# Later places for z transposes, v's split, the routing gate and the first block table in a fused attention, MLP and mixture-of-experts kernel

## The chip, the cores and the metric

One core of a Trainium2 chip. The metric is the device time of one execution in microseconds (us). TensorE (PE) does the matmuls and transposes, with a weight loader of its own (PEld); VectorE (DVE), ScalarE (ACT) and GpSimd (POOL) do the elementwise work; SyncE (SP) issues most DMAs, GpSimd the indirect ones. Every engine runs its own instructions in program order.

## What is computed

Three stages over 8 batches of 3072 rows of 256 columns, all float32:

```
scores = (z @ z.T) / S                     # z: 3072 x 64 in each batch
x      = u * (relu(scores)**2 @ v)         # attention
h      = x @ w_in                          # 256 -> 2048
x      = (h - tanh(h)) @ w_out             # 2048 -> 256
e      = argmax(x @ w_gate)                # 8 experts, one for each row
gate   = softmax(x @ w_gate)[e] * sigmoid((x @ w_output_gate)[e])
out    = gate * (relu(x @ w1[e]) @ w2[e])  # 256 -> 1024 -> 256
```

To keep float32's precision, each operand of most products is split into a high part (rounded to the matmul's type) and a low part (operand minus high part), and three products (high by high, high by low, low by high) are summed.

## The kernel before

**Stages.** The rows go in 48 chunks of 512 (NCH; 6 in a batch, NG). Chunk c has twelve steps p (NJP), each over 256 keys: `s_mm` (scores into PSUM), `s_relu` (relu and square, ScalarE), `s_split` (high part "a" on VectorE, or on ScalarE for p=1 and 7; low part on GpSimd for p=0, 2, 4, 6, 8, 9, 10, else on VectorE) and `av_mm` (times v). Then `x_make` multiplies by the transposed u and splits x. The MLP of chunk c-1 runs between the steps of chunk c: for each of eight blocks f of w_in and w_out, `wi_mm` (h into PSUM), `g_first`, `g_second`, `g_third` (h - tanh h, by ScalarE and VectorE) and `wo_mm`. Chunk c-2 is then routed, also between the steps of chunk c: `x2_split`, `g_mm` (logits), `route1` (argmax, one-hot), `route2` (positions: five small matmuls "prs", a copy "cum", then six VectorE instructions, among them the cast to whole numbers "pi", L577), `route_gate` (two Exps on ScalarE, L538 and L543, and seven small VectorE instructions), `rows_out` (the rows with their gate to DRAM), `ids_out` (four indirect DMAs that put row numbers into a table sorted by expert). When all chunks are routed, blocks of one expert's rows are gathered and multiplied; the first 39 blocks have 512 rows, the rest 256. The table that tells each block its expert and start is made in two halves by `block_table` from single-partition VectorE work: `table_counts`, `table_steps`, `table_expert` (eight times), `table_out`.

**Order.** No planner: every function is entered by `at(t, fn, ...)` with a time written out by hand (in `SCHED` and the loops), all entries are sorted by that time, and the instructions are issued in this order. So a later time moves a function behind others on every engine's queue that it uses, SP's and GpSimd's too. A chunk is 88 of these units long, a step 7.33. `gap(c, k)` is the time 3.4 units into step k of chunk c.

**Around the change.** In the last chunk of each batch (c = 11, 17, ...) the next batch's z and v come in: `z_load`, `z_split` (GpSimd), `z_tr` (four transposes, then a ScalarE copy to t1, L312), `v_load`, `v_split` (high part on ScalarE, L332; low part on GpSimd, L336). PSUM holds one score tile ("sc"), one h tile and the accumulators; the score tile is also used by `z_tr`, by `u_tr` (the transposes of u, after the scores of p=8), by `g_mm` and by `route2`. The order of a mid-batch chunk c around the routing, before the change:

```
s_mm(c,6) s_relu(c,6) route_gate(c-2) rows_out(c-2) wi_mm(c-1,3,0) s_split(c,6) route2(c-2)
wi_mm(c-1,3,1) ids_out(c-2,0) av_mm(c,5) e_load g_first(c-1,3) s_mm(c,7) wo_mm(c-1,2,0)
g_second(c-1,3) s_relu(c,7) wo_mm(c-1,2,1) g_third(c-1,3) s_split(c,7) av_mm(c,6) wi_mm(c-1,4,0)
s_mm(c,8) s_relu(c,8) wi_mm(c-1,4,1) s_split(c,8) g_first(c-1,4) u_tr(c)
```

`g_third(c-1,2)` stands ahead of this, so its four VectorE instructions come before those of route_gate. The functions that the diff touches, with the lines of the profile:

Of the kernel before, what the change touches and what calls it, by code (L numbers as in the profile page):

```python
# [21 lines left out]
LGC = 128  # L22

SCHED = dict(
    TC=88.0, LA=1.8, EX=3.4, UT=8, ZS=12.0, ZL=(1, 2, 7, 9, 11, 13), M0=0.5, HI=2.5, LG=1.45,
    HA=((1, 3, 5, 7, 9, 11), (1, 2, 4, 5, 7, 8, 10, 11), (1, 7)), LP=((), (6, 8, 10), (0, 2, 4, 6, 8, 9, 10)),
    G2=3.0, G3=5.0, GT=180.0, CT=((16.0, 23.0), (36.0, 43.0), (56.0, 63.0), (76.0, 83.0), (98.4, 102.0), (110.5, 120.4), (131.5, 142.4), (153.5, 155.4)),
    CP=(34.5, 54.5, 74.5, 98.3, 109.4, 131.4, 149.0, 164.3),
# [36 lines left out]
def build(tc, u, v, z, w_in, w_out, w_gate, w_ogate, w1, w2, out):  # L65
# [5 lines left out]
    E = w_gate.shape[1]  # L71
    F2 = w1.shape[2]
    NG = S // CH
    NCH = B * NG
    NJP = S // 256
# [17 lines left out]
    def at(t, fn, *a):  # L93
        tasks.append((t, len(tasks), fn, a))
# [59 lines left out]
    with ExitStack() as st:  # L154
# [53 lines left out]
        T1, T4, V, UT, X, X2, AVP, XP, WS = {}, {}, {}, {}, {}, {}, {}, {}, {}  # L208
        RR, AA, HH, GG, ROWS, LG, GT = {}, {}, {}, {}, {}, {}, {}
# [387 lines left out]
        K = SCHED  # L597
        TC = K["TC"]
        DJ, DF = TC / NJP, TC / NFP
        LA = K["LA"] * DJ  # L600
        EX = K["EX"]

        def gap(c, k):

            c, k = c + k // NJP, k % NJP
            return c * TC + k * DJ + EX

        T_ROUTED = {}
        for b in range(B):
            for g in range(NG):  # L610
                if b == 0:
                    tz = -60.0 + g * K["Z0"]
                    tzt, tv = tz + 2, K["VT"][g]
                else:
                    t0 = (b * NG - 1) * TC
                    tzt, tv = gap(b * NG - 1, K["ZL"][g]), t0 + (2 * g - 1) * DJ + LA + 3.0
                    tz = tzt - K["ZS"]
                at(tz - 9 if b else -75.0 + g, z_load, b, g)
                at(tz, z_split, b, g)
                at(tzt, z_tr, b, g)  # L620
                at(tv - (12 if b else 20 if g else 10), v_load, b, g)
                at(tv, v_split, b, g)
# [9 lines left out]
        for n, c in enumerate([c for c in range(3, NCH - 3) if c % NG != NG - 1][: 4 * E]):  # L632
            t = c * TC + K["ES"]
            at(t - 20.0, e_load, n // 4, n // 2 % 2, n % 2)
            at(t, e_split, n // 4, n // 2 % 2, n % 2)
        for c in range(NCH):
            t0 = c * TC
            at(t0 - (14 if c else 45), t4_make, c)
            at(t0 + TC / 4, u_load, c)
            at(gap(c, K["UT"] * NJP // 12), u_tr, c)  # L640
            for p in range(NJP):
                t = t0 + p * DJ
                at(t, s_mm, c, p)
                at(t + 1.0, s_relu, c, p)
                at(t + 3.0, s_split, c, p)
                at(t + LA, av_mm, c, p)
            end = c == NCH - 1
            at(t0 + TC + LA + 3.0 + K["XM"] if end else t0 + (TC - DJ) + LA + 3.0, x_make, c)
            tm0 = t0 + TC + LA + K["M0"]
            for f in range(NFP):  # L650
                t = tm0 + f * DF
                at(t - (22 if c else 10), ws_load, c, f)
                for i in range(2):
                    at(t + i * K["HI"], wi_mm, c, f, i)
                    lag = K["LG"] * DF + i * K["HI"]
                    if c == NCH - 2 and f == NFP - 1:

                        lag = tm0 + TC + K["W7"] + 0.1 * i - t
                    at(t + lag, wo_mm, c, f, i)
                at(t + K["HI"] + 1.5, g_first, c, f)  # L660
                at(t + K["HI"] + K["G2"], g_second, c, f)
                at(t + K["HI"] + K["G3"], g_third, c, f)
            te = tm0 + (NFP - 1 + K["LG"]) * DF + K["HI"] + 1.5
            if c == NCH - 2:
                te = tm0 + TC + K["W7"] + 1.0
            at(te, x2_split, c)

            n = int((te + 4.0 - EX - t0) // DJ) + 1

            tx, tx1, tx2 = (gap(c, n + h) for h in range(3))  # L670
            tx2 += K["RX"] if end else 0.0
            if c == NCH - 2:

                tx, tx1, tx2 = (t0 + 2 * TC + LA + 3.0 + x for x in K["R6"])
            at(tx, g_mm, c, 0)
            at(tx1, g_mm, c, 1)
            tr = tx1 + (K["R1"] if c == NCH - 2 else 1.5)
            at(tr, route1, c)
            tg = tr + (0.01 if c >= NCH - 2 else 4.0)
            at(tg, route_gate, c)  # L680
            at(tg + 0.5, rows_out, c)
            at(tx2 + (0.5 if c >= NCH - 2 else 1.5), route2, c)

            io = K["IO3"] if c == NCH - 3 else K["IO"]
            for t_ in range(4):
                at(tx2 + (1.0 if c >= NCH - 2 else 2.0) + t_ * io, ids_out, c, t_)
            T_ROUTED[c] = tx2 + 1.0 + 3 * io
# [74 lines left out]
                tt(used[:, 0:E], end, sta, op=ALU.subtract)  # L762

        def block_table(t, half, d):

            at(t, table_counts, half)
            at(t + 2.0 * d, table_steps, half)
            for e in range(E):
                at(t + (4.0 + e) * d, table_expert, half, e)
            at(t + 13.0 * d, table_out, half)  # L770
            return t + 13.0 * d
# [187 lines left out]
        at(170.0, more_consts)  # L959
        at(K["GT"], gates)  # L960
        at(200.0, table_consts)
        t_table = T_ROUTED[NCH - 3] if NA else T_ROUTED[NCH - 1] - 13.0

        block_table(t_table + K["TB0"] - 3 * K["IO3"], 0, K["TBD"])
        t_table = block_table(T_ROUTED[NCH - 1] + 0.2, 1, 1.0)
        tC = NCH * TC + LA + 3.0

        def when(n):

            T, d = K["TS"], 22.0 / (NF2 // 2)  # L970
            k = int(n)
            at_ = lambda k: T[k] if k < len(T) else T[-1] + (k - len(T) + 1) * d
            return tC + at_(k) + (n - k) * (at_(k + 1) - at_(k))

        t0 = when(0)
# [3 lines left out]
        for i in range(NA + NHB):  # L979
            TB = 22.0 if i < NA else 11.0  # L980
            if i == NA:
                t0 = max(t0 + 5.5, t_table + 50.0)
# [33 lines left out]
            t0 = step(NG2) if i + 1 < NA or i >= NA else step(0) + TB  # L1016
# [46 lines left out]
```

## Time and profile before

| | |
|---|---|
| median of 3 runs | 5629.36 us (5626.49 to 5629.8) |
| the profiled execution | 5628.64 us |
| its span, first to last instruction | 5626.9 us |
| TensorE busy | 5564.5 us (99%) |
| VectorE, ScalarE, GpSimd busy | 4255.2, 3576.4, 1794.5 us |
| TensorE's granted clock, mean | 0.997 |

The profile is of one execution. Times in the rows are us from the start of the span. A row of the timeline has start, duration, engine, line of the kernel, operation, output<-inputs with their shapes, the number of instructions merged (x1), and in brackets how long the engine had been idle ahead of it and whose end released it. Matmuls are pipelined, so they overlap in the rows: one of 512 columns lasts 0.39 and the next begins about 0.23 after it.

### The profile page before, as it was taken

What the parts mean: (1) busy time and instruction counts of PE and PEld (TensorE: products, weight loads), DVE (VectorE), ACT (ScalarE), POOL (GpSimd) and SP (SyncE); (2) the same over time, 40 slices, a digit from 0 to 9 for tenths busy, and PEclk for the clock granted to TensorE, in tenths of its full rate; (3) what the DMA queues carried; (4) which work ended last, traced back from release to release, by engine and by line L of the source; (5) the groups of instructions that cost most, each with busy time, mean ns of one, the idle gap of its engine ahead of it and who ended that gap; (6) DMA issues with size and microseconds to landing.
All of it is one profiled execution on the core that took longest, in us unless ns stands there. A gap on an engine that the chain in (4) does not pass through costs nothing. (4 is left out here: it accounts for less than half of the span.)

```text
span 5626.9 us, 71022 instructions
## 1 busy us (share of the span) xinstructions
PE 5564.5 (99%) x26788; PEld 4635.4 (82%) x26788; DVE 4255.2 (76%) x5119; ACT 3576.4 (64%) x3990; POOL 1794.5 (32%) x1170
## 2 busy tenths in 40 slices
PE   8899999999999999999999999999999999999999
PEld 7788888888888888888888888888888888888898
DVE  8788888888888888888888888888888733333344
ACT  8677776777777777767777776777766432223344
POOL 1224222432333233222423332333222233333365
PEclk9999999999999999999999999999999999999999
DMA  6334333333433333334334333333333666666688
GB/s 213 108 123 140 127 129 125 138 128 122 134 130 132 123 131 130 130 120 145 127 119 136 136 125 130 121 141 117 106 113 110 218 223 230 231 232 230 229 298 299
DMA packets 192472, 872.06 MB, mean 155 GB/s; under 512 B 37178, under 2 KB 78272, under 8 KB 128640
## 3 DMA queue, kind: packets, MB, share of 16 engines
q1 hardware_dynamic: 154384, 763.19, 39.2%
q0 software_dynamic: 37312, 103.92, 5.4%
q8 instruction: 213, 3.49, 0.3%
q14 instruction: 131, 1.07, 0.1%
q10 hardware_dynamic: 432, 0.39, 0.0%
HBM read 757.16 MB, written 98.96 MB: 152 GB/s over the span
## 5 line engine op out<-in xcount | busy, mean ns | idle before, releaser
L385 POOL TENSOR_TENSOR a<-r,a 128x1024 fp32r<-128x1024 f32 x325 | 783.9, 2412 | 2578.8 <-DVE a L382 1997.7
L371 ACT ACTIVATE r<-sc 128x1024 f32<-128x1024 f32 x576 | 588.1, 1021 | 943.4 <-PE sc L366 941.2
L432 PE MATMUL h<-x,ws 128*128 128x512 f32 x4608 | 1160.4, 392 | 13.0 <-issue 5.7
L468 PE MATMUL x<-g,ws 128*128 128x512 f32 x4608 | 1150.7, 392 | 2.4 <-DVE g L457 1.4
L432 PEld LDWEIGHTS h<-x,ws 128*128 128x128 f32 x4608 | 862.5, 188 | 199.7 <-issue 11.7
L468 PEld LDWEIGHTS x<-g,ws 128*128 128x128 f32 x4608 | 856.8, 188 | 181.9 <-DVE g L458 5.2
L403 PE MATMUL av<-a,v 128*128 128x512 f32 x2304 | 901.3, 391 | 14.5 <-DVE ut L411 9.8
L404 PE MATMUL av<-a,v 128*128 128x512 f32 x2304 | 898.6, 390 | 0.0
L894 DVE SCALAR_TENSOR_TENSOR hh<-h,hh 128x1024 fp32r<-128x1024 f32 (+1 forms) x248 | 254.6, 1027 | 581.4 <-ACT hh L893 564.7
L372 ACT ACTIVATE r<-r 128x1024 f32<-128x1024 f32 x576 | 611.6, 1062 | 18.3
L406 PE MATMUL av<-a,v 128*128 128x512 f32 x2304 | 616.7, 389 | 2.3 <-POOL a L385 2.3
L882 PE MATMUL h<-xt,b 128*128 128x512 f32 (+1 forms) x2976 | 607.8, 353 | 0.1
L439 DVE TENSOR_TENSOR gd<-h,gd 128x1024 f32<-128x1024 f32 x384 | 468.2, 1219 | 168.7 <-ACT gs L438 168.7
L893 ACT ACTIVATE hh<-h 128x1024 fp32r<-128x1024 f32 (+1 forms) x248 | 215.2, 868 | 592.3 <-PE h L882 440.6
L454 DVE SCALAR_TENSOR_TENSOR gq<-gt,gq 128x1024 f32<-128x1024 f32 x384 | 539.4, 1405 | 54.8 <-ACT gt L449 30.0
L382 DVE CAST a<-r 128x1024 fp32r<-128x1024 f32 x470 | 359.3, 764 | 248.1 <-ACT r L372 163.9
L455 DVE COPY_PREDICATED gq<-gm,gd 128x1024 f32<-128x1024 uint16 x384 | 534.6, 1392 | 13.2
L882 PEld LDWEIGHTS h<-xt,b 128*128 128x128 f32 x2976 | 479.0, 189 | 77.4 <-DVE xt L866 0.5
L403 PEld LDWEIGHTS av<-a,v 128*128 128x128 f32 x2304 | 433.4, 188 | 107.1 <-DVE ut L411 10.2
L406 PEld LDWEIGHTS av<-a,v 128*128 128x128 f32 x2304 | 432.7, 188 | 93.2 <-POOL a L385 3.0
L404 PEld LDWEIGHTS av<-a,v 128*128 128x128 f32 x2304 | 433.4, 188 | 88.9
L458 DVE TENSOR_TENSOR g<-gq,g 128x1024 fp32r<-128x1024 f32 x384 | 476.6, 1241 | 13.1
(158 smaller groups left out, 8570.9 us busy)
## 6 DMA issues: line engine op xcount, KB each, us to landing
ws<-wsd SPq DMA_DIRECT2D x384, 1024.0 KB
b<-wsp SPq DMA_DIRECT2D x102, 2048.0 KB
wsp<-el POOLq DMA_DIRECT2D x32, 1024.0 KB
x2d<-rows SPq DMA_DIRECT2D x48, 576.0 KB
wr<-in_moe_w SPq DMA_DIRECT2D x25, 1024.0 KB
vr<-in_v SPq DMA_DIRECT2D x48, 512.0 KB
ur<-in_u SPq DMA_DIRECT2D x48, 512.0 KB
er<-in_moe_w SPq DMA_DIRECT2D x32, 512.0 KB
```

The lines of the kernel that those rows point to most:

```text
L371: nc.scalar.activation(r, RR.pop((c, p)), AF.Relu, scale=1.0 / S)
L372: nc.scalar.activation(r, r, AF.Square)
L385: eng.tensor_tensor(a[:, 1], r, a[:, 0].bitcast(F32), op=ALU.subtract)
L403: nc.tensor.matmul(dst, vh, a[:, 0, k], start=(J == 0), stop=False)
L404: nc.tensor.matmul(dst, vl, a[:, 0, k], start=False, stop=False)
L406: nc.tensor.matmul(dst, vh, a[:, 1, k], start=False, stop=(J == 2 * NJP - 1))
L432: nc.tensor.matmul(ps, w, x[:, l, k], start=(n == 0), stop=(n == 5))
L454: nc.vector.scalar_tensor_tensor(q, s, pk, q, op0=ALU.add, op1=ALU.mult)
L455: nc.vector.copy_predicated(q, m.bitcast(U16), d)
L458: nc.vector.tensor_sub(gg[:, 1], q, gg[:, 0].bitcast(F32))
L468: nc.tensor.matmul(XP[c][d], w, gg[:, l, i], start=first and n in (0, 2), stop=last and n > 3,)
L882: nc.tensor.matmul(ps[:, j], b1[a][:, k, f * P : (f + 1) * P], xt[:, l, k, 0:W], start=(n == 0 and (W == CH or j == 0)), stop=(n == 3 * ND ...
```

## The change

Five edits of the order; no instruction is added or removed:

- the z transposes of g=2 go from 7 to 7.45 steps into the last chunk of a batch, and with them their load and split (all 3.3 units later);
- `v_load` and `v_split` of a batch's first group (g=0) are 4 units later;
- the last `s_split` (c=47, p=11) is 0.1 later, which puts it behind `g_first(46,6)`;
- `route_gate` and `rows_out` of chunks 0 to 45 are 4.2 units later: behind `s_split(c,6)`, `route2` and the first `ids_out`, `rows_out` also behind an `e_load`, and still ahead of `g_first(c-1,3)`;
- the first half of the block table, spread before over 19.5 units, goes in three lots: counts behind `g_first(46,3)`; steps and experts 0 to 3 behind `g_third(46,3)`; experts 4 to 7 and the output behind `g_first(46,4)`, ahead of `g_third(46,4)`.

With the change the order of the same stretch, and in the last chunk of a batch with z_tr, is:

```
s_mm(c,6) s_relu(c,6) wi_mm(c-1,3,0) s_split(c,6) route2(c-2) wi_mm(c-1,3,1) ids_out(c-2,0)
route_gate(c-2) av_mm(c,5) e_load rows_out(c-2) g_first(c-1,3) s_mm(c,7) wo_mm(c-1,2,0)
g_second(c-1,3) s_relu(c,7) [v_split(b,3)] wo_mm(c-1,2,1) g_third(c-1,3) s_split(c,7) av_mm(c,6)
wi_mm(c-1,4,0) [z_tr(b,2)] s_mm(c,8) s_relu(c,8) ...
```

(before, `z_tr(b,2)` stood behind `s_split(c,7)`, ahead of `av_mm(c,6)`).

```diff
@@ -22,7 +22,7 @@
 LGC = 128
 
 SCHED = dict(
-    TC=88.0, LA=1.8, EX=3.4, UT=8, ZS=12.0, ZL=(1, 2, 7, 9, 11, 13), M0=0.5, HI=2.5, LG=1.45,
+    TC=88.0, LA=1.8, EX=3.4, UT=8, ZS=12.0, ZL=(1, 2, 7.45, 9, 11, 13), M0=0.5, HI=2.5, LG=1.45,
     HA=((1, 3, 5, 7, 9, 11), (1, 2, 4, 5, 7, 8, 10, 11), (1, 7)), LP=((), (6, 8, 10), (0, 2, 4, 6, 8, 9, 10)),
     G2=3.0, G3=5.0, GT=180.0, CT=((16.0, 23.0), (36.0, 43.0), (56.0, 63.0), (76.0, 83.0), (98.4, 102.0), (110.5, 120.4), (131.5, 142.4), (153.5, 155.4)),
     CP=(34.5, 54.5, 74.5, 98.3, 109.4, 131.4, 149.0, 164.3),
@@ -613,7 +613,7 @@
                     tzt, tv = tz + 2, K["VT"][g]
                 else:
                     t0 = (b * NG - 1) * TC
-                    tzt, tv = gap(b * NG - 1, K["ZL"][g]), t0 + (2 * g - 1) * DJ + LA + 3.0
+                    tzt, tv = gap(b * NG - 1, K["ZL"][g]), t0 + (2 * g - 1) * DJ + LA + (3.0 if g else 7.0)
                     tz = tzt - K["ZS"]
                 at(tz - 9 if b else -75.0 + g, z_load, b, g)
                 at(tz, z_split, b, g)
@@ -638,13 +638,13 @@
             at(t0 - (14 if c else 45), t4_make, c)
             at(t0 + TC / 4, u_load, c)
             at(gap(c, K["UT"] * NJP // 12), u_tr, c)
+            end = c == NCH - 1
             for p in range(NJP):
                 t = t0 + p * DJ
                 at(t, s_mm, c, p)
                 at(t + 1.0, s_relu, c, p)
-                at(t + 3.0, s_split, c, p)
+                at(t + (3.1 if end and p == NJP - 1 else 3.0), s_split, c, p)
                 at(t + LA, av_mm, c, p)
-            end = c == NCH - 1
             at(t0 + TC + LA + 3.0 + K["XM"] if end else t0 + (TC - DJ) + LA + 3.0, x_make, c)
             tm0 = t0 + TC + LA + K["M0"]
             for f in range(NFP):
@@ -676,7 +676,7 @@
             at(tx1, g_mm, c, 1)
             tr = tx1 + (K["R1"] if c == NCH - 2 else 1.5)
             at(tr, route1, c)
-            tg = tr + (0.01 if c >= NCH - 2 else 4.0)
+            tg = tr + (0.01 if c >= NCH - 2 else 8.2)
             at(tg, route_gate, c)
             at(tg + 0.5, rows_out, c)
             at(tx2 + (0.5 if c >= NCH - 2 else 1.5), route2, c)
@@ -762,7 +762,13 @@
                 tt(used[:, 0:E], end, sta, op=ALU.subtract)
 
         def block_table(t, half, d):
-
+            if not half:
+                at(tC - 53.2, table_counts, half)
+                at(tC - 49.95, table_steps, half)
+                for e in range(E):
+                    at(tC - (49.9 if e < E // 2 else 42.4) + 0.1 * e, table_expert, half, e)
+                at(tC - 41.5, table_out, half)
+                return tC - 41.5
             at(t, table_counts, half)
             at(t + 2.0 * d, table_steps, half)
             for e in range(E):
@@ -959,11 +965,11 @@
         at(170.0, more_consts)
         at(K["GT"], gates)
         at(200.0, table_consts)
+        tC = NCH * TC + LA + 3.0
         t_table = T_ROUTED[NCH - 3] if NA else T_ROUTED[NCH - 1] - 13.0
 
         block_table(t_table + K["TB0"] - 3 * K["IO3"], 0, K["TBD"])
         t_table = block_table(T_ROUTED[NCH - 1] + 0.2, 1, 1.0)
-        tC = NCH * TC + LA + 3.0
 
         def when(n):
 
```

## Rows read from the trace of the kernel before

**Rows 1.** The page, part 1: busy time, share of the span, instructions.

```profile
PE 5564.5 (99%) x26788; PEld 4635.4 (82%) x26788; DVE 4255.2 (76%) x5119; ACT 3576.4 (64%) x3990; POOL 1794.5 (32%) x1170
```

**Rows 2.** The table of waits: engine, line, waited for: us in total, times, longest.

```profile
ACT sm L543 <- DVE sm L542: 113.3, 47, 3.2
...
PEld ups L351 <- ACT r L371: 11.3, 47, 0.2
```

**Rows 3.** Timeline of ScalarE in mid-batch, chunk c=14.

```profile
1407.34 0.20 ACT L543 ACTIVATE sm<-sm 128x4 f32<-128x4 f32 x1 [2.28 <-DVE sm L542]
...
1407.54 1.02 ACT L437 ACTIVATE gd<-h 128x1024 f32<-128x1024 f32 x1
...
1417.13 1.03 ACT L371 ACTIVATE r<-sc 128x1024 f32<-128x1024 f32 x1 [2.33 <-PE sc L366]
```

**Rows 4.** Timeline of VectorE, the same stretch.

```profile
1406.60 0.18 DVE L539 TENSOR_TENSOR ex<-lg,oh 128x32 f32<-128x32 f32 x1
...
1407.14 0.17 DVE L542 TENSOR_SCALAR sm<-sm 128x4 f32<-128x4 f32 x1
...
1408.10 0.69 DVE L382 CAST a<-r 128x1024 fp32r<-128x1024 f32 x1
...
1408.93 0.19 DVE L575 TENSOR_TENSOR pos<-pos,oh 128x32 f32<-128x32 f32 x1
...
1409.37 2.05 DVE L577 CAST pi<-pf 128x4 int32<-128x4 f32 x1
...
1411.48 1.21 DVE L439 TENSOR_TENSOR gd<-h,gd 128x1024 f32<-128x1024 f32 x1
```

**Rows 5.** Timeline of GpSimd, the same stretch.

```profile
1408.94 2.45 POOL L385 TENSOR_TENSOR a<-r,a 128x1024 fp32r<-128x1024 f32 x1 [13.40 <-DVE pos L574]
```

**Rows 6.** All instructions of line 577: duration ns min/median/max, first and last start.

```profile
L577 DVE CAST pi<-pf x48: 169/2036/2291, 224.8 to 4541.5; 128x4 int32<-128x4 f32 x48
```

**Rows 7.** Timeline of TensorE, the same stretch.

```profile
1416.87 1.52 PE L432 MATMUL h<-x,ws 128*128 128x512 f32 x6
1418.23 1.08 PE L351 MATMUL ups<-ident,ur 128*128 128x128 f32 x8
```

**Rows 8.** Timeline of TensorE at a batch end, chunk c=11.

```profile
1002.51 2.03 PE L432 MATMUL h<-x,ws 128*128 128x512 f32 x6
...
1007.30 1.99 PE L468 MATMUL x<-g,ws 128*128 128x512 f32 x6
```

**Rows 9.** The same batch end: VectorE, then GpSimd.

```profile
1000.90 3.08 DVE L415 TENSOR_TENSOR x<-ut,x 128x512 fp32r<-128x512 f32 x2 [2.10 <-ACT x L414]
...
1000.43 2.41 POOL L336 TENSOR_TENSOR v<-vr,v 128x1024 fp32r<-128x1024 f32 x1 [1.38 <-ACT v L332]
```

**Rows 10.** The same batch end, steps 7 and 8: TensorE, then ScalarE.

```profile
1049.01 0.51 PE L306 MATMUL zps<-identr,za 128*128 128x128 f32 x4 [1.11 <-ACT r L371]
...
1053.59 0.39 PE L365 MATMUL sc<-t,t 128*128 128x512 f32 x1
...
1051.76 0.58 ACT L312 ACTIVATE t<-zps 128x512 fp32r<-128x512 f32 x1
```

**Rows 11.** Batch end: two issues of SP, then GpSimd's split of z.

```profile
979.33 1.68 SPq L286 DMA_DIRECT2D zr<-in_z  x1
...
1037.18 0.33 SPq L422 DMA_DIRECT2D ws<-wsd  x1
...
988.05 0.40 POOL L295 CAST za<-zr 128x256 fp32r<-128x256 f32 x1 [0.66 <-DMA zr<-in_z]
```

**Rows 12.** Timeline of VectorE in the last attention chunk.

```profile
4339.17 0.23 DVE L744 TENSOR_SCALAR tb_cmp<-it,tb_end 1x40 f32<-1x40 f32 x1
...
4342.37 0.67 DVE L382 CAST a<-r 128x1024 fp32r<-128x1024 f32 x1
...
4362.02 2.10 DVE L382 CAST a<-r 128x1024 fp32r<-128x1024 f32 x1 [0.93 <-issue]
```

## The prediction

> **What bounds the kernel now.** I read part 1 of the page first: TensorE is busy 5564.5 of 5626.9 us [rows 1], so all the gaps that any edit could close are 62 us, the start included. Then the table of waits: ScalarE waits 113.3 us, 47 times, for one instruction, the routing's second Exp ("sm"), and TensorE's weight loader waits 47 times for a relu in front of the u transposes ("ups") [rows 2]. So the question is whether ScalarE comes too late for TensorE, and I went to the timelines of one chunk in mid-batch (c=14, where chunk 12 is routed) [rows 3 to 7], of one at a batch end (c=11) [rows 8 to 11], and of the last attention chunk [rows 12].
>
> In mid-batch TensorE has no gap at all, but one place has no slack either. The score tile has one PSUM buffer. wi's six matmuls start at 1416.87 and the transposes of u, which overwrite the scores of p=8, follow at 1418.23 [rows 7]; the relu that frees them starts at 1417.13 and lasts 1.03, to 1418.16 [rows 3]. So whatever makes that relu later moves TensorE by as much. The relu itself has a reserve: ScalarE idled 2.33 us ahead of it [rows 3].
>
> At a batch end there are gaps. wi(10,0,0) takes 2.03 where six such matmuls take 1.52, and wo(9,7,0) 1.99 [rows 7, 8]: x's low part took 3.08 on VectorE while GpSimd made v's low part from 1000.43 [rows 9]. And the z transposes wait 1.11 for a relu [rows 10].
>
> **The change, part by part.**
>
> *route_gate 4.2 later (46 chunks).* It goes from between g_third and s_split(c+2,6) to behind route2, still ahead of g_first. On VectorE the stretch from s_split's cast (1408.10) to g_first's subtraction (1411.48), 3.38 us, now runs first, and the gate's seven small instructions after it [rows 4]. The stretch is so long because of one CAST, pi, of 4 columns: 2.05 us [rows 4], held until GpSimd's pass over a's low part ends (1408.94 + 2.45 = 1411.39, rows 5). It takes 0.169 at its fastest [rows 6]. GpSimd's pass is set off by the cast itself, 0.84 after it, so both move ahead together and the hold stays. Thus sm, which follows the gate's third instruction, comes at 1407.34 + 3.38 = 1410.72 [rows 3, 4]. Behind it on ScalarE stand tanh and the square for g_first, g_second's two passes, relu and square for p=7, the Copy of a(7), and the relu of p=8, each without a gap. What leaves the stretch is the copy of route2's counts (about 0.1 of the 0.20 between sm and tanh) and an overlap of issue of about as much. Lateness of the relu for p=8: 3.38 - 2.33 - 0.17 = 0.88 us, and so much later the u transposes start. h's buffer for wi(13,4,0) and the score buffer for p=8 also open later, but ahead of that gate, and are contained in it. After it ScalarE and VectorE stand to TensorE about as before, so the loss comes once a chunk. 46 routings less 7 at batch ends and the last: 38 x 0.88 = **+33.4 us**. Bounds: 0.5 a chunk (twice the overlaps I took) and 1.3 (0.43 more, see the second rival). rows_out moves with the gate behind an e_load on SP: nothing waits for x2d before the second stage, cost nothing.
>
> *z transposes of g=2, 3.3 later (7 batch ends), and the gate there.* Before, the transposes wait 1.11 at 1049.01, and the scores of p=8 start at 1053.59 [rows 10]. Now they stand directly ahead of those scores and share their buffer, so the scores wait for the copy t1 (L312), which on ScalarE is behind everything sm holds up. It ran at 1051.76, 0.58 long [rows 10]. With sm 3.38 later and less 0.1 for the counts' copy: it starts at 1055.04 and ends at 1055.62, and the scores start at about 1055.7, **+2.1** against 1053.59. The 1.11 are in this. The load of z on SP now comes behind a load of MLP weights (issued at 1037.18); one that came so landed some 8.7 after its issue (979.33 to 988.05) [rows 11]. The split is ahead of a's low part on GpSimd's queue, so it may hold that up: from 0 to 1.2 (its two passes meeting VectorE's cast). Should it land so late that pi gets in ahead of GpSimd, sm comes earlier instead. I take +0.3: 2.4, ends 0.2 and 3.3.
>
> *v's low part 4 later (7 batch ends).* v's high part leaves ScalarE's queue ahead of x_make (1 us), and GpSimd's pass no longer meets x's low part. That ends wi's 0.51. By the durations in the rows the pass now starts near 1003, when I expect VectorE in g_third; the cast after it may be held by GpSimd instead. So of wo's 0.47 I take 0.3: gain 0.8, between 0.5 and 1.0. The load swaps places with a z load on SP, about 0.5 us, hidden by the twelve units of lead. Where page and row meet: x's low part (two SBUF inputs, beside GpSimd) was slowed to 3.08 [rows 9]. The Trainium skill, "SBUF — State Buffer", section "Who interferes with whom", states that whichever of the two starts first has the shared ports for its whole instruction and the other waits; the 3.08 agree with it. By this rule the hold moves to g_third's cast rather than going away, and the gain would be nearer 0.5.
>
> Batch end together: 7 x (2.4 - 0.8) = **+11 us**.
>
> *Block table and the last s_split.* Five experts took 4339.17 to 4342.37 [rows 12], 0.64 each. The counts get out of the way of the h that follows, but four experts and the output, about 3.8 us, now stand ahead of g_third(46,4), on which wo waits. Moving the last s_split behind g_first(46,6) frees wi(46,7) of a CAST of 2.10 [rows 12]. Ends -3 and +3; I take **+1**, as the added stretch is the longest.
>
> Sum: 33.4 + 11 + 1 = 45.4. The profiled execution took 5628.64 (span 5626.9); its median stands 0.7 higher at 5629.36. So 5629.4 + 45.4 = about **5675 us**. A measurement of this kernel tells some 0.2%, 11 us, from no change.
>
> **Rivals.**
>
> *Not slower: pi isn't held.* If GpSimd's pass falls behind the small cast in the new order, the stretch shrinks by 2.05 - 0.17 = 1.9, sm is only 1.5 late, and the 2.33 of reserve cover it. The point from which it decides is a sm later by 2.4. Then mid-batch costs nothing, and a batch end gains about 0.6: 5629.4 - 4 + 1 = 5626. For it: the shortest of the 48 casts shows that pi by itself is small [rows 6]. Against it: the cast that starts the pass keeps its distance to pi. Chance 0.08.
>
> *Slower by more.* Between cast and pi stands a multiply with two SBUF inputs (L575), which starts at 1408.93, 0.01 ahead of GpSimd's pass at 1408.94 [rows 4, 5]. If it loses that race it is held for the whole pass, and the reduction and pi come after it: 0.43 more (1409.37 - 1408.94) in 45 chunks, 19 us, 5694. The Trainium skill, the same page and section, counts such an instruction among those that wait; [rows 9] agree. Nothing changes the distance, so 0.06.
>
> *Faster.* The gate proves harmless and the batch ends lose all of 0.51 + 0.47 + 1.11, 15 us: 5614. For it: those gaps are real. Against: it needs the t1 copy hidden, where nothing stands between the transposes and the scores any more. Chance 0.06.
>
> **How the numbers follow.** The forecast has 0.80, "by more" 0.06, no difference 0.08, faster 0.06. Slower by over 0.2%: 0.86. Range: the low end takes 0.5 x 38 + 0.5 x 7 - 3, 19.5: 5649. The high end 1.1 x 38 + 2.5 x 7 + 3, 62, plus a little of the second rival: 5694. Both other cases lie below it.
>
> **What would show it.** In the changed trace, mid-batch: ScalarE's wait ahead of sm grows from 2.3 to 5 us or more, sm comes after pi, pi still lasts 2.04, the idle ahead of the relu for p=8 is gone, and a gap of 0.9 us stands in front of the u transposes, released by that relu, 38 times. At batch ends x's low part takes 1.3 and wi 1.52, but the scores of p=8 wait for t1. I am wrong if pi is short, or if the relu of p=8 still waits for TensorE. TensorE's granted clock should not move.

## The result and the profile after

The changed kernel takes 5696.84 us, median of 4 runs (5696.02 to 5697.81), against 5629.52 us for the kernel before on the same chip: a ratio of 1.0122 with a 95% interval of 1.0109 to 1.0136. It is 67 us slower where 45 were forecast: the sign is right, and the time lies 3 us above the range. The profiled execution took 5697.81 us with a span of 5696.1, 69.2 more than before.

The page, part 1, and two rows of the table of waits (engine, line, waited for: us in total, times, longest), beside [rows 1, 2]:

```profile
PE 5583.9 (98%) x26788; PEld 4640.5 (81%) x26788; DVE 4289.5 (75%) x5119; ACT 3571.4 (63%) x3990; POOL 1789.1 (31%) x1170
...
POOL a L385 <- DVE a L382: 2584.8, 302, 29.3
...
ACT sm L543 <- DVE sm L542: 283.8, 47, 7.7
```

The counts of instructions are the same. ScalarE waits 283.8 us for the second Exp, where it waited 113.3, so one wait has grown by 170 us. TensorE's own part of the table shows what of that reached it:

```profile
PE h L432 <- PE av L406: 29.7, 38, 0.8
...
PE sc L365 <- ACT t L312: 11.5, 7, 2.3
```

38 gaps in front of a wi_mm, one in each mid-batch chunk, and 7 in front of scores, one at each batch end.

**Mid-batch.** The same chunk as before (c=14), some 20 us later in the span by now. ScalarE, VectorE, GpSimd and TensorE, beside [rows 3, 4, 5, 7]:

```profile
1432.16 0.20 ACT L543 ACTIVATE sm<-sm 128x4 f32<-128x4 f32 x1 [5.88 <-DVE sm L542]
1432.27 1.01 ACT L437 ACTIVATE gd<-h 128x1024 f32<-128x1024 f32 x1
...
1427.72 0.68 DVE L382 CAST a<-r 128x1024 fp32r<-128x1024 f32 x1
1428.33 0.18 DVE L574 TENSOR_TENSOR pos<-cum,run 128x32 f32<-128x32 f32 x1
1428.54 2.39 DVE L575 TENSOR_TENSOR pos<-pos,oh 128x32 f32<-128x32 f32 x1
...
1431.18 0.17 DVE L577 CAST pi<-pf 128x4 int32<-128x4 f32 x1
...
1435.37 1.22 DVE L441 SCALAR_TENSOR_TENSOR gq<-h,gs 128x1024 f32<-128x1024 f32 x1
...
1428.49 2.39 POOL L385 TENSOR_TENSOR a<-r,a 128x1024 fp32r<-128x1024 f32 x1 [11.80 <-DVE a L382]
...
1436.68 1.63 PE L432 MATMUL h<-x,ws 128*128 128x512 f32 x6 [0.79 <-PE av L406]
...
1440.47 1.09 PE L351 MATMUL ups<-ident,ur 128*128 128x128 f32 x8
```

What to see: pi is short (0.17), but the multiply L575 is held for 2.39, as long as GpSimd's pass. The pass starts 0.77 after the start of the cast L382, 0.05 ahead of the multiply; before, it started 0.84 after the cast and 0.01 behind the multiply [rows 4, 5]. The multiply itself keeps its distance to the cast (0.82 after, 0.83 before).

Why the pass comes sooner can't be read from the brackets. They name the cast now (a L382) and the addition L574 (pos) before [rows 5], but they go by the semaphore event that came last, and the pass doesn't use what L574 makes. The trace also holds the instructions in which an engine only waits for a semaphore. Those of GpSimd at line 385 in the whole kernel before, then in the changed one; then the one of the stretch before, with VectorE's L574 there:

```profile
L385 POOLq EVENT_SEMAPHORE  x51: 17/17/43, 109.2 to 4325.5; - x51
...
L385 POOLq EVENT_SEMAPHORE  x5: 17/17/43, 111.0 to 210.1; - x5
...
L385 POOLq EVENT_SEMAPHORE  x1: 17/17/17, 1408.8 to 1408.8; - x1
...
1408.71 0.18 DVE L574 TENSOR_TENSOR pos<-cum,run 128x32 f32<-128x32 f32 x1
```

Before, 46 more passes than after have a waiting instruction of their own ahead of them, for VectorE. In c=14 it was over at 1408.85, behind the end of the cast (1408.79) and ahead of the end of L574 (1408.89): the cast lets the pass go in both orders. Before, the pass then carried a further wait, for ScalarE. In the changed kernel the cast carries the wait for ScalarE, and the pass itself the one for VectorE. So it is in every kernel of this study in which the pass stands in its old place: with the gate ahead of the cast the pass waits for ScalarE and starts 0.84 after the cast (median), with the gate behind the cast it doesn't and starts 0.77 after it. That the pass can do without this wait because the cast now has it is an inference from these lists of waits.

All instructions of the two lines (ns min/median/max, first and last start), beside [rows 6]:

```profile
L575 DVE TENSOR_TENSOR pos<-pos,oh x48: 191/2382/2392, 224.1 to 4610.5; 128x32 f32<-128x32 f32 x48
...
L577 DVE CAST pi<-pf x48: 170/170/367, 226.8 to 4611.0; 128x4 int32<-128x4 f32 x48
```

So sm comes 4.44 after the start of this cast (1432.16 - 1427.72). Before, VectorE's first instruction of the gate in that place, L539, was 0.74 ahead of sm [rows 3, 4]: sm is 3.70 later. TensorE's gap stands at wi(13,4,0), which starts 0.09 after g_first's last reading of the h tile that it overwrites (L441, 1435.37 + 1.22 = 1436.59), and not at the u transposes. The 0.79 counts from the modelled end of the matmul before. From start to start, wi comes 1.86 after av's last four matmuls (1436.68 - 1434.82) where it came 0.91 after them before, and its own six take 0.11 longer: 1.06 of the 1.14 us that a chunk loses.

**The last chunk of a batch.** VectorE, GpSimd and TensorE in the first steps of c=11, then GpSimd, VectorE, ScalarE and TensorE in its steps 6 to 8, beside [rows 8 to 11]:

```profile
1013.29 1.29 DVE L415 TENSOR_TENSOR x<-ut,x 128x512 fp32r<-128x512 f32 x2 [1.10 <-ACT x L414]
1017.16 2.74 DVE L457 CAST g<-gq 128x1024 fp32r<-128x1024 f32 x1
1016.24 3.11 POOL L336 TENSOR_TENSOR v<-vr,v 128x1024 fp32r<-128x1024 f32 x1 [3.84 <-ACT v L332]
1015.85 1.52 PE L432 MATMUL h<-x,ws 128*128 128x512 f32 x6
1019.95 1.99 PE L468 MATMUL x<-g,ws 128*128 128x512 f32 x6
...
1055.08 0.74 POOL L295 CAST za<-zr 128x256 fp32r<-128x256 f32 x1 [6.61 <-DMA zr<-in_z]
1055.47 0.89 DVE L382 CAST a<-r 128x1024 fp32r<-128x1024 f32 x1
1057.03 2.32 DVE L575 TENSOR_TENSOR pos<-pos,oh 128x32 f32<-128x32 f32 x1
1060.58 0.21 ACT L543 ACTIVATE sm<-sm 128x4 f32<-128x4 f32 x1 [7.46 <-DVE sm L542]
1065.10 2.50 PE L432 MATMUL h<-x,ws 128*128 128x512 f32 x6 [2.37 <-issue]
1069.26 0.79 PE L365 MATMUL sc<-t,t 128*128 128x512 f32 x1 [1.19 <-ACT t L312]
```

x's low part takes 1.29 instead of 3.08 and wi(10,0,0) 1.52 instead of 2.03, but wo still 1.99, because g_third's cast (L457, normally 0.69) is held for 2.74 by the pass over v that now meets it. At the end of the chunk z's split waits 6.61 for its load, lies beside the cast (0.89 instead of 0.69), and the multiply is held again, as at six of the seven ends: sm comes 5.11 after the start of the cast (1060.58 - 1055.47), 4.37 more than 0.74. TensorE then waits twice, 2.37 and 1.19: for h's buffer, which g_first's last reading frees, and for t1. The windows of that end (stretch, us, busy us and count of PE, PEld, DVE, ACT, POOL, then granted clock as a share of 2.4 GHz, DMA share, GB/s):

```profile
1062.00:1066.00 4.00, 1.63 (x7) 1.06 (x6) 3.25 (x3) 3.94 (x5) 0.00 (x0) 0.95 0.99 298
1066.00:1069.00 3.00, 2.07 (x8) 1.39 (x7) 2.90 (x4) 3.00 (x4) 1.14 (x1) 0.50 0.97 228
1069.00:1073.00 4.00, 3.74 (x10) 2.98 (x11) 4.00 (x2) 1.74 (x3) 3.92 (x3) 0.58 0.10 41
```

In the stretch with the first gap TensorE was busy for 1.63 of 4 us; then its granted clock was 0.50, the lower level of 1.2 GHz, for 6.8 us, and six wi matmuls took 2.50 instead of 1.52. Two of the seven batch ends have such a stretch of 6.8 us, two one of 3.4 us, three none.

**Where the 69 us are.** The first prs matmul of each routing marks one point in each chunk. The table is the time from one mark to the next, less the same time of before; the groups add up to the difference of the spans.

| periods | change each, us | together |
|---|---|---|
| 30 in mid-batch | 1.14 (median) | 34.6 |
| 8 with the first half of a batch's last chunk, the last one without v's split | 0.39 to 0.80 (seven), 1.14 | 4.6 |
| 7 with a batch end | 3.14, 5.11, 3.05, 3.19, 5.93, 3.35, 3.23 | 27.0 |
| the last two | 1.87, 0.03 | 1.9 |
| before the first mark, after the last | 1.47, -0.34 | 1.1 |

The two ends above 5 are those with 6.8 us at the lower clock. The time before the first mark varies from -1.2 to +1.5 over the kernels of this study and is not explained by any edit.

### The profile page after: what moved, and what is told of

Same layout as the page of the kernel before. It is cut to its first block, busy times and chain, and to the rows that moved or that the text cites. A ratio compares the mean times of both kernels' runs of the same rounds, so it can differ in the third digit from the quotient of the medians.

```text
span 5696.1 us, 71005 instructions
## 1 busy us (share of the span) xinstructions
PE 5583.9 (98%) x26788; PEld 4640.5 (81%) x26788; DVE 4289.5 (75%) x5119; ACT 3571.4 (63%) x3990; POOL 1789.1 (31%) x1170
## 5 line engine op out<-in xcount | busy, mean ns | idle before, releaser
L382 DVE CAST a<-r 128x1024 fp32r<-128x1024 f32 x470 | 361.9, 770 | 250.1 <-ACT r L372 173.0
L455 DVE COPY_PREDICATED gq<-gm,gd 128x1024 f32<-128x1024 uint16 x384 | 519.2, 1352 | 13.2
```

The source lines that it names most:

```text
L455: nc.vector.copy_predicated(q, m.bitcast(U16), d)
```

## The experiments

Each ran beside the kernel before (5627.01 us in the first group, 5628.14 in the second, 5626.19 in the last). In the tables of this section "mid" is the median change of a mid-batch period, "first half" and "end" the mean of the seven periods with the first half of a batch's last chunk and with its end, as above.

| run | time, us | ratio, 95% interval | mid | first half | end |
|---|---|---|---|---|---|
| the change | 5696.84 | 1.0122 (1.0109 to 1.0136) | 1.14 | 0.49 | 3.86 |
| gate alone | 5715.55 | 1.0156 (1.0139 to 1.0173) | 1.17 | 1.23 | 6.01 |
| all but the gate | 5626.26 | 0.9997 (0.9987 to 1.0006) | 0.00 | -0.71 | 0.67 |
| both ahead | 5637.22 | 1.0017 (1.0008 to 1.0027) | 0.01 | -0.37 | 1.45 |
| z loaded early | 5695.99 | 1.0122 (1.0105 to 1.0139) | 1.16 | 0.54 | 3.85 |
| pass behind ids | 5648.27 | 1.0034 (1.0023 to 1.0045) | 0.24 | -0.21 | 1.57 |
| v and the end | 5623.16 | 0.9990 (0.9981 to 0.9999) | 0.00 | -0.68 | 0.03 |
| gate split | 5625.17 | 0.9995 (0.9986 to 1.0004) | -0.01 | -0.01 | -0.44 |
| v, end, gate split | 5621.25 | 0.9987 (0.9978 to 0.9996) | 0.00 | -0.71 | -0.52 |
| pass later | 5694.50 | 1.0121 (1.0104 to 1.0138) | 1.03 | 0.38 | 4.58 |

**Gate alone, and all but the gate.** The kernel before with the gate's edit only, and the changed kernel without it:

```diff
-            tg = tr + (0.01 if c >= NCH - 2 else 4.0)
+            tg = tr + (0.01 if c >= NCH - 2 else 8.2)
```

> The kernel before with route_gate and rows_out 4.2 units later and nothing else. Theory: the gate's second Exp now comes behind a multiply of route2 that GpSimd's pass over a's low part holds for 2.4 us, ScalarE stands behind it, and TensorE waits in front of wi(c-1,4,0): 38 mid-batch chunks at 1.13 us, 43 us, and at the 7 batch ends about 3 us each, because the z transposes wait for a relu that is 3.7 us later: 60 to 68 us, 5690 to 5698. Rival: the batch ends get their loss from the later z transposes, the later z load and the block table: then 43 to 48 us, 5672 to 5678.

> The changed kernel with route_gate at its old place. Theory: no mid-batch gap; at a batch end v's later split gives back 0.6 to 0.8 us, and of the z transposes' later place a part is lost again: 5618 to 5632, same as the kernel before or a little below. Rival (the later z work costs by itself): the copy t1 in front of the scores and the late z load cost 1.5 to 2.5 us at each of 7 batch ends: 5640 to 5648.

The gate alone costs more than the whole change, and more than was expected of it: mid-batch came as expected, but a batch end cost 6.0 where some 3 were. Without the gate nothing is left that can be told from no change. TensorE's waits with the gate alone, then with all but the gate:

```profile
PE zps L306 <- ACT r L371: 36.7, 7, 5.4
PE h L432 <- PE av L406: 29.7, 37, 0.8
```

```profile
PE sc L365 <- ACT t L312: 4.8, 7, 0.7
```

The mid-batch gap belongs to the gate entirely. The parts are not additive at the batch ends: where the z transposes keep their early place, they wait up to 5.4 for the relu behind the late sm, and an end costs 6.0; their later place saves 2.1 of that (6.01 - 3.86). Without the late gate the same place costs 0.6 (0.67 against 0.03 in "v and the end"): the transposes' wait of 1.11 is gone, but the scores wait 0.7 for t1, and other scores 0.7 for route2's copy, where they waited 0.2 before.

**Both ahead.** Does the loss come from the gate's place behind route2, or from its place behind the cast that lets GpSimd's pass go? Here the order route2, gate is that of the changed kernel, but both stand ahead of s_split(c,6):

```diff
-            tg = tr + (0.01 if c >= NCH - 2 else 8.2)
+            tg = tr + (0.01 if c >= NCH - 2 else 5.3)
...
-            at(tx2 + (0.5 if c >= NCH - 2 else 1.5), route2, c)
+            at(tx2 + (0.5 if c >= NCH - 2 else -0.65), route2, c)
```

> The changed kernel with route2 and then route_gate put together ahead of s_split(c,6), so that the gate stays behind route2, but the cast that sets off GpSimd's pass comes after both. Theory (the loss comes from GpSimd's hold of route2's multiply or cast): pi and the multiply last 0.2 each, the second Exp is 1.3 us later than before the change instead of 3.7, the reserve of 2.4 covers it, no mid-batch gap: 5615 to 5635. Rival (the gate behind route2's six instructions is too late in itself, held or not): the mid-batch gap stays at 0.5 to 1.1 us, 5650 to 5690.

Its mid-batch, VectorE:

```profile
1411.00 0.19 DVE L575 TENSOR_TENSOR pos<-pos,oh 128x32 f32<-128x32 f32 x1
...
1411.44 0.17 DVE L577 CAST pi<-pf 128x4 int32<-128x4 f32 x1
...
1413.18 0.69 DVE L382 CAST a<-r 128x1024 fp32r<-128x1024 f32 x1
```

Nothing ahead of the second Exp is held, and the median loss per chunk is 0.01. So it is the place behind the cast, with GpSimd's pass beside it, and not the order of route2 and the gate. The mean loss is 0.16: some chunks lose up to 0.7 in front of another wi_mm, and the cause of that is open. The time lies 2 us above the range that was expected, because the ends still cost 1.45. They also show what the lower clock costs. All seven have the same gap of 1.74 to 1.77 in front of the scores; the five with a stretch of 3.4 us at the lower clock behind it cost 1.65 to 2.43, the two without one 0.17 and 0.24.

**z loaded early.** The wait of 6.61 for z at the batch end looked like a cause of its loss. The changed kernel with this load 3.3 units earlier, where it was before:

```diff
-                at(tz - 9 if b else -75.0 + g, z_load, b, g)
+                at(tz - (12.3 if g == 2 else 9) if b else -75.0 + g, z_load, b, g)
```

> The changed kernel with only the load of z for g=2 put back to its old time (the split and the transposes stay late). Theory: at the batch ends GpSimd's split of z is done before the cast of a(6), the second Exp comes 0.6 to 1.2 us earlier than in the changed kernel, the gaps there shrink by as much and TensorE's clock doesn't drop: 8 to 14 us less than the changed kernel, 5683 to 5689. Rival (the landing of z isn't what is late, the batch end is as slow as the mid-batch gate makes it): within 3 us of the changed kernel.

The time is the same, so the theory fell in its sum. GpSimd's wait for z (in the changed kernel 52.8 us in 14) is nearly gone:

```profile
POOL za L295 <- DMA zr<-in_z: 6.5, 7, 2.7
```

The two gaps of the batch end of c=5, where the granted clock stays up in both kernels, in the changed kernel and then here:

```profile
509.71 1.61 PE L432 MATMUL h<-x,ws 128*128 128x512 f32 x6 [2.37 <-issue]
...
513.87 0.50 PE L365 MATMUL sc<-t,t 128*128 128x512 f32 x1 [2.25 <-ACT t L312]
...
506.60 1.63 PE L432 MATMUL h<-x,ws 128*128 128x512 f32 x6 [1.73 <-issue]
...
510.76 0.50 PE L365 MATMUL sc<-t,t 128*128 128x512 f32 x1 [2.24 <-ACT t L312]
```

The first gap is 0.64 shorter and the second the same, so the late load does have a price: the two ends without the lower clock cost 2.55 and 2.59 here, the three of the changed kernel 3.05 to 3.35. But five ends have a stretch at the lower clock here, one of them 6.8 us long, and cost 4.11 to 4.62 each. The gain and this loss cancel. Why the clock falls at more of the ends here is not shown.

**Pass behind ids.** If the held small instructions are the cause, moving GpSimd's pass over a's low part (p=6) behind the first ids_out, and nothing else, should bring the time back:

```diff
+            if p == 6 and c >= 2:
+                LOW[c] = (a, r)
+                return
             eng.tensor_tensor(a[:, 1], r, a[:, 0].bitcast(F32), op=ALU.subtract)
...
+                if p == 6 and c >= 2:
+                    at(t + 5.45, low_late, c)
```

> The changed kernel with one instruction moved: GpSimd's pass over a's low part for p=6 comes behind the first ids_out on GpSimd's queue, which itself needs the end of route2, so the pass can't hold route2's or the gate's small instructions. VectorE's and ScalarE's orders are those of the changed kernel. Theory (the hold makes the loss): multiply and pi at 0.2, the second Exp 1.8 us later than before the change instead of 3.7, covered by the reserve: no mid-batch gap, 5620 to 5645. Rival (the gate's place behind cast and route2 on VectorE and ahead of g_first on ScalarE is too late by itself): a mid-batch gap of 0.3 us or more stays, 5650 to 5690.

Mid-batch in this kernel (its lines behind 385 stand 9 higher, so L584 is L575, L586 is L577, L554 is L545, a step of the gate behind the second Exp):

```profile
1415.14 0.19 DVE L584 TENSOR_TENSOR pos<-pos,oh 128x32 f32<-128x32 f32 x1
...
1415.59 0.17 DVE L586 CAST pi<-pf 128x4 int32<-128x4 f32 x1
...
1416.80 2.86 DVE L554 TENSOR_SCALAR sm<-sm 128x4 f32<-128x4 f32 x1 [0.20 <-ACT sm L552]
...
1416.18 0.99 POOL L598 DMA_INDIRECT table<-ids,pi  x1 [12.94 <-PE av L415]
1417.19 2.43 POOL L395 TENSOR_TENSOR a<-r,a 128x1024 fp32r<-128x1024 f32 x1
```

The hold has moved to an instruction of 4 columns behind the second Exp, which ScalarE doesn't wait for. It starts ahead of the pass, while GpSimd's first indirect DMA runs, and ends with the pass; which of the two held it first is not shown. VectorE and ScalarE run what they ran in the changed kernel, in that order, and the loss goes from 1.14 to 0.24 a chunk: the hold ahead of the Exp is four fifths of it. The 0.24 go with the new hold: g_first's subtraction stands behind L554 on VectorE and starts at 1420.01, though ScalarE's square, for whose end it waited in the changed kernel, had ended at 1418.59, and the same wi_mm follows 0.10 after g_first's last reading. The time (5648.27) lies between the two that were expected.

**v and the end; gate split; both.** Is there a version that gains? "v and the end" is the kernel before with v's split later, the table in lots and the last s_split. "Gate split" is the kernel before with the gate cut in two: the first Exp and its three VectorE instructions stay, the second Exp and the rest go 5.35 units later, behind g_first:

```diff
             nc.vector.tensor_scalar(sm[:, 1], sm[:, 1], -88.5, None, op0=ALU.max)
+
+        def route_gate2(c):
...
             nc.scalar.activation(sm[:, 1], sm[:, 1], AF.Exp, scale=-1.0)
...
             at(tg, route_gate, c)
+            tg += 0.0 if c >= NCH - 2 else 5.35
+            at(tg, route_gate2, c)
```

> The kernel before with v's later load and split, the three lots of the block table and the later last s_split; the gate and the z transposes as before. Theory: 0.7 us at each of 7 batch ends come back (5), 2 at the end: 5618 to 5622. Rival (these moves give nothing without the z transposes' move): within 2 us of the kernel before.

> The kernel before with the gate cut in two: its first Exp and three VectorE instructions stay, the second Exp and the rest come behind g_first, 5.35 units later. Theory (ScalarE standing at the second Exp is what makes the batch ends' gap in front of the z transposes): that wait goes from 2.3 to near 0, the 1.1 and 0.4 us at the batch ends go, mid-batch unchanged: 5614 to 5622. Rival (that gap has another cause, or the second half delays g_second): within 3 us of the kernel before, or 5640 and more if the second half stands behind something held.

> Both of the two before together: v's split, table lots and last s_split of the change, and the gate cut in two at its old place. Theory: the gains add up, 12 to 20 us: 5607 to 5616. Rival: the one hides the other, 5616 to 5624.

v's later split is worth 0.68 a batch, 4.8 us in all; the 2 us that were also expected of the table and the last s_split did not come. One line shows it, x's low part in "v and the end" (x96: busy us, mean ns, then VectorE's idle time ahead of them); before it was 74.6 and 819:

```profile
L415 DVE TENSOR_TENSOR x<-ut,x 128x512 fp32r<-128x512 f32 x96 | 62.1, 688 | 52.3 <-ACT x L414 52.2
```

The split gate takes away the z transposes' wait of 1.11 [rows 10], and gives half of it back a little later, in front of a wo_mm whose g comes late because another small instruction is held. Its batch end, VectorE and TensorE:

```profile
1047.19 2.23 DVE L548 TENSOR_SCALAR sm<-sm 128x4 f32<-128x4 f32 x1
...
1053.71 1.99 PE L468 MATMUL x<-g,ws 128*128 128x512 f32 x6 [0.58 <-DVE g L457]
```

The split gate alone was expected at 5614 to 5622 us and came to 5625.17, the same as the kernel before. Together the two give 5621.25 us, 0.13% below it, where a sum of the gains was expected to reach 5607 to 5616. That is the fastest version of the study, and less than the 0.2% that a measurement can tell with safety.

**Pass later.** Last, the lost race by itself. In the changed kernel a small GpSimd instruction, the first 32 columns of the same subtraction done twice, goes ahead of the pass, so that the multiply should win again:

```diff
+            if p == 6 and c >= 2:
+                eng.tensor_tensor(a[:, 1, 0, 0:32], r[:, 0, 0:32], a[:, 0, 0, 0:32].bitcast(F32), op=ALU.subtract)
             eng.tensor_tensor(a[:, 1], r, a[:, 0].bitcast(F32), op=ALU.subtract)
```

> The changed kernel, with one small GpSimd instruction (the first 32 columns of the same subtraction, computed twice) put ahead of GpSimd's low pass of p=6, so that the pass starts some 0.1 to 0.3 us later and the multiply L575 is ahead of it again. If the lost race is the second part of the loss: L575 takes 0.19 again in most of the 48 routings, pi is held 2.0 again, sm comes about 0.43 earlier in mid-batch, and the loss per mid-batch chunk falls from 1.14 to 0.7 to 0.9 (the forecast had 0.88), the time from 5696.8 by 38 x 0.25 to 38 x 0.43 to some 5680 to 5687. If what the hold costs depends only on when GpSimd's pass ends and not on which small instruction it catches: L575 short, but sm where it was and 1.14 a chunk, 5697. If the small instruction itself catches L575 and the pass follows at its heels, the multiply stays held and the run says nothing of the race: 5697 with L575 at 2.4 or more.

Mid-batch in this kernel (lines behind 385 stand 2 higher: L577 is the multiply, L579 is pi, L545 is the second Exp):

```profile
1424.80 0.69 DVE L382 CAST a<-r 128x1024 fp32r<-128x1024 f32 x1
...
1425.57 0.25 POOL L386 TENSOR_TENSOR a<-r,a 128x32 fp32r<-128x32 f32 x1 [11.83 <-DVE a L382]
...
1425.62 0.24 DVE L577 TENSOR_TENSOR pos<-pos,oh 128x32 f32<-128x32 f32 x1
...
1426.12 2.19 DVE L579 CAST pi<-pf 128x4 int32<-128x4 f32 x1
...
1425.90 2.39 POOL L387 TENSOR_TENSOR a<-r,a 128x1024 fp32r<-128x1024 f32 x1
...
1429.12 0.20 ACT L545 ACTIVATE sm<-sm 128x4 f32<-128x4 f32 x1 [5.76 <-DVE sm L544]
```

The multiply lost to the small instruction (1425.57), which held it by some 0.05, and won against the pass. The hold went back to pi, yet the loss fell only from 1.14 to 1.03, where 0.7 to 0.9 was expected. The pass starts 1.10 after the cast here, 0.33 later than in the changed kernel (0.77) and 0.26 later than before (0.84), so the hold ends later by as much. sm comes 4.32 after the cast (1429.12 - 1424.80) instead of 4.44. From the end of the pass it comes 0.83 later here (1429.12 - 1428.29) and 1.28 in the changed kernel (1432.16 - 1430.88), so the lost race by itself costs 0.45, near the 0.43 of the forecast's rival; the earlier start of the pass gives 0.07 of it back. With the pass where it was before and the race won, sm would be at 4.06 by these numbers (4.32 - 0.26), 3.32 later than 0.74. That is an estimate; the race was not undone without moving the pass. By it the lost race has 0.38 of sm's 3.70, and the other 3.32 are near the 3.38 that the forecast had without it.

The ends in this run cost 4.58, 0.7 more than in the changed kernel although sm is earlier. All seven have a stretch at the lower clock, three of them 6.8 us long. Of the four with 3.4 us, two have it between the two gaps and cost 3.0, two behind the second gap and cost 5.2 and 5.9.

## Why the prediction was right in sign and too low

**The direction and the mechanism held.** The gate costs what it costs because its second Exp stands in ScalarE's queue behind VectorE instructions that GpSimd's pass holds. "All but the gate", "both ahead" and "pass behind ids" show it from three sides. The forecast's 38 places and the wait ahead of sm "5 us or more" are in the trace (5.88). TensorE waits for what is late behind sm.

**The step that failed** is "GpSimd's pass is set off by the cast itself, 0.84 after it, so both move ahead together and the hold stays", with "Nothing changes the distance" in the second rival. The cast does set the pass off, in both orders, but the distance was not a fixed one: in the changed order the pass no longer waits for ScalarE besides, starts 0.77 after the cast, and the multiply loses by 0.05 a race that it had won by 0.01. No row of before showed that this wait would go; that 0.01 is a thin lead they did show. So the rival that was given 0.06 happened on top of the forecast. sm is 3.70 later instead of 3.38. A chunk loses 1.14 instead of 0.88: 38 x 1.14 = 43.3 against 33.4, 9.9 of the 22 us that were missed. The forecast had itself put the upper bound of a chunk at 1.3, for this rival, but added up its range with 1.1; with 1.3 the range would have held the measured time.

The rule that the forecast cited holds for the multiply in both orders. The Trainium skill, "SBUF — State Buffer", section "Who interferes with whom", says that the order of issue decides which of the two blocks. The kernel before and the changed one agree: the multiply took 0.19 when it started ahead of the pass and 2.39 when it started behind it.

**Where the loss surfaces** was a miss of place. The forecast took the gate for h's buffer as contained in the gap at the u transposes. The gap stands there, at wi(13,4,0) (0.79), and the u transposes follow without one. It is one lateness of ScalarE seen at an earlier gate, so no second price.

**The batch ends were mis-sized.** The forecast had 2.4 a piece less 0.8 for v, +11 in all. Measured are 27.0 for the ends less 4.8 for v's split (7 x 0.68), 22.2: the other 11 us of the miss. v's part came out near: 0.68 against 0.8, and by the same rule of the Trainium skill, since g_third's cast is now held (2.74) and wo still takes 1.99. The end itself cost 3.86 instead of 2.4. Three things went into it. sm is 4.37 later and not 3.38: the race again, z's split beside the cast (0.89 for 0.69) and the addition (0.72 for 0.18). TensorE waits twice, ahead of wi and ahead of the scores, where the forecast had one wait. And the granted clock fell to its lower level behind these gaps, although the forecast said that it should not move, and put no price on it. The two ends with 6.8 us at it cost 5.11 and 5.93, the other five 3.05 to 3.35, so about 4.6 of the 27 us go with it (5.11 + 5.93 - 2 x 3.2). "Both ahead" shows the price by itself, 1.4 to 2.3 us for a stretch of 3.4. Where such a stretch lies between the two gaps it costs next to nothing, since the slowed matmuls then fill the second gap: in the changed kernel the end of c=23 has it there, its second gap is 1.09 instead of 2.25, and it cost 3.19. Why the clock fell at some ends and not at others is not shown.

**The table and the last s_split** were forecast at +1. The last two periods and the tail hold 1.9 - 0.3 = 1.6, and of the 1.87 in the first of them the gate alone has 1.47. So they cost next to nothing; "v and the end" has 0.27 there.

**The other rivals.** "pi isn't held" came true in its condition, which was also the forecast's sign of being wrong, and not in its result: pi took 0.17, and the hold sat on the multiply two instructions ahead of it. "Faster" needed t1's copy hidden; the scores wait for it at all seven ends.

## What to carry to other kernels

Do not assume that two instructions on different engines keep their distance when a third is moved: the move can change which waits stand in front of them. Here one wait less made a pass 0.07 earlier, and that decided a race with a lead of 0.01. A bracket names the event that came last; check it against what the instruction reads. A short instruction in an in-order queue is priced with what can hold it: here 128x4 casts and 128x32 products each cost a whole pass of another engine, and an Exp that waited for them held all of ScalarE behind it. Moving such a chain behind the instruction that sets off the long pass is what cost 1.1 us a chunk; ahead of it, the same chain cost 0.01 in the median.

## What the runs showed of the hardware

- A VectorE instruction of 4 or 32 columns can be held for a whole pass of GpSimd, and the hold moves from one to another: 2.39 for L575 (0.19 in the kernel before), 2.19 for pi (0.17 in the changed kernel), 2.86 for a TENSOR_SCALAR of 128x4 (0.17 before, 0.35 in the changed kernel), each until GpSimd's pass of 2.4 had ended. Not each small one is: the reduction between the multiply and pi took 0.19 in "pass later" while the pass ran.
- GpSimd's pass, let go by the same cast, started 0.84 after it with a waiting instruction of its own ahead of it, 0.77 without.
- Idle times of TensorE at the batch ends went with 3.4 or 6.8 us at a granted clock of 0.50, at some ends and not at others: at 4 of 7 in the changed kernel (two gaps, 2.1 to 2.6 and then up to 2.25), 5 of 7 in "both ahead" (one gap of 1.75), 7 of 7 with the gate alone (one of 5.2 to 5.4) and in "pass later", none in "all but the gate" (two of 0.7).
